# Moving work between engines at the head of an attention and gated feed-forward kernel: normalisation shared with ScalarE, second products placed behind their own unit, the weights' check moved to the end

## The chip, the cores and the metric

One core of one Trainium2 chip runs the whole program. The metric is the device time of one execution in microseconds (us). The engines are TensorE (PE, whose weight loads are listed as PEld), VectorE (DVE), ScalarE (ACT), GpSimd (POOL) and SyncE (SP), which issues nearly all DMAs. Every engine works through its own queue of instructions in order; semaphores hold an instruction until what it reads is ready.

## What is computed

```
scores = q k^T / 8 + bias(head, distance), kept for the last 96 keys and 8 global ones
a      = exp(scores - max) ;  a = a / (sum(a) + 1e-9) ;  x = a v      (4 x 8 heads x 768 x 64)
h      = relu(x @ w_in)                                               (4 x 768 x 1024)
gate   = sigmoid(conv over 3 neighbouring rows of h, weights conv_w)
out    = (h * gate) @ w_out                                           (4 x 768 x 512)
```

The weights arrive as 64-bit floats. The kernel decodes them on the chip from their two 32-bit words, and checks that every high word lies in the range that the short decoding covers; a flag at the very end chooses a general path if one does not. The profiled path is the fast one.

## The kernel before

A *unit* is half of one batch's rows: 384 rows, 8 units (n = 0 to 7). Attention runs in 96 *steps*: step s handles 128 query rows of one pair of heads, three steps make one pair (m), and twelve steps make a unit. In step s PE computes the scores of both heads into one PSUM tile (`scores`, tile s, two buffers), DVE adds the bias and takes the minimum of the negated scores (`maxima`, L378), ACT takes the exponential with its sum (`exps`, L390, into one of three buffers pbuf). `normalise` then runs: DVE adds 1e-9 to the two sums (L398) and takes the reciprocals (L399), POOL multiplies head 0 and head 1 (L402, twice). PE transposes the result (t, L410 and L411), ACT evacuates it (pt, L417), and every third step PE multiplies by v (pv, L433), with ACT and DVE splitting the result into a high and a low part (xh L445, xl L446).

A unit's feed-forward work is built by `ffn(n)` as a list of pieces, which `fill` spreads over the following twelve steps. First products: for each of eight feature blocks f, 12 matmuls (h, L464; tile h1_0 is unit 1, block 0), then relu on ACT (hbuf, L474). The convolution `conv` follows some blocks later: one multiply on POOL (L510), two multiply-adds on DVE (L511, L512). `gate` is a tanh on ACT for two blocks at a time (L530) and `saturated` a test of it, also on ACT (L541). `split` multiplies by h on DVE (L563, tile c), rounds to a high part on ACT (gh, L565) and subtracts on DVE (gl, L566). Second products `mm2`: 24 matmuls for each tile of 128 rows (o, L575; tile o0_2 is batch 0, rows 256 to 383), evacuated by ACT (ob) and stored.

Before the change, `ffn(n)` holds the second products of the tiles that unit n - 1 has completed. Unit 0 has none of its own behind it, so the rest of its convolutions, gates and splits is kept in a list `late` and handed to unit 1's first products, one piece per block. Unit 1's list then contains tiles o0_0 and o0_1, unit 2's list the four tiles o0_2 to o0_5.

Steps 0 to 10 stand in the order in which the code was written (`manual_schedule`); from step 11 on a scheduler of the library orders each engine's queue. Lists of chores ("dve", "pool", "act") are worked off with a budget in every step. They decode the 16 pieces of the weights (w_in first, then w_out: DVE L290, L292, L294, POOL L299, DVE L305), each loaded by SP in 512 KB (tile wr, four buffers). The "act" chores check each piece while it lies there: `piece_check` squares the high words with their sum (L312) and clamps the squares (L315). `check_weights` and `check_gates` turn the results into the flag.

Of the kernel before, what the change touches and what calls it, by code (L numbers as in the profile page):

```python
# [20 lines left out]
P = 128  # L21
# [14 lines left out]
NPB = 3  # L36
HAND = 11
# [25 lines left out]
def fast_path(tc, io):  # L63
# [243 lines left out]
    def piece_check(i, half, n):  # L307
        k = 2 * i + half
        if n == 0:
            squares[k] = p1.tile([P, HW], F32, tag="ob", name=f"square{k}")  # L310
            x = wraw[i, half][:, :, 1].bitcast(F32)
            A.activation(squares[k], x, AF.Square, accum_out=chk[:, NCHK + k : NCHK + k + 1])  # L312
        else:
            y = squares[k]
            A.activation(  # L315
                y, y, AF.Relu, bias=least, scale=-(2.0**30), accum_out=chk[:, k : k + 1]
            )

    squares = {}
# [65 lines left out]
    def exps(s):  # L385
        m, i = steps[s]
        sp, c0, n, mm = st_s[s]
        pb = pbuf[s % NPB]
        for j in range(2):
            last_exp[s] = A.activation(  # L390
                pb[:, j, c0 : c0 + n], sp[j][:, c0 : c0 + n], AF.Exp,
                bias=mm[:, j : j + 1], scale=-1.0, accum_out=mm[:, 2 + j : 3 + j],
            )
        st_s[s] = (pb, c0, n, mm)

    def normalise(s):
        pb, c0, n, mm = st_s[s]
        V.tensor_scalar(mm[:, 4:6], mm[:, 2:4], 1.0e-9, None, ALU.add)  # L398
        V.reciprocal(mm[:, 6:8], mm[:, 4:6])  # L399
        for j in range(2):  # L400
            x = pb[:, j, c0 : c0 + n]
            G.tensor_scalar(x, x, mm[:, 6 + j : 7 + j], 1.0, ALU.mult, ALU.mult)  # L402
# [189 lines left out]
    late = []  # L592

    def ffn(n, defer=True):
        items = []
        add = lambda cost, fn, *a: items.append((cost, fn, a))
        early, lag = late[:], 1 + len(late) // 2
        late.clear()
        for f in range(NF):
            for part in range(3):  # L600
# [17 lines left out]
        old = tiles_of(n - 1) if n else []  # L618
# [43 lines left out]
    chores = {"dve": [], "pool": [], "act": []}  # L662
# [50 lines left out]
    for s in range(len(steps) + LAG_V + 1):  # L713
        cur["s"] = s
        m, i = steps[s] if s < len(steps) else (len(jobs), -1)
        if s < HAND:
# [26 lines left out]
            work("act", 0.8)  # L743
        else:
# [53 lines left out]
    fill(10**9)  # L798

# [14 lines left out]
    def general():  # L814
# [27 lines left out]
        for n in range(NU):  # L842
# [31 lines left out]
            for _, fn, a in ffn(n, defer=False):  # L874
                fn(*a)
# [98 lines left out]
```

## Time and profile before

| what | value |
|---|---|
| median of 3 runs | 479.29 us (476.66, 479.29, 855.67) |
| the profiled execution | 476.23 us, of which the traced span is 474.4 us |
| mean granted TensorE clock in it | 0.959 |
| PE, DVE, ACT, POOL busy, share of the span | 96%, 75%, 62%, 53% |
| HBM read and written | 44.68 MB and 6.29 MB |

The shares are averages over stages with different limits. Matmuls overlap in PE's pipeline, and their ends are modelled, so that a PE which is busy all the time may still wait between matmuls. Tables by stretches of time therefore tell more here than the shares.

### The profile page before, as it was taken

How to read it: one execution, taken by the hardware profiler on the slowest of the kernel's cores; microseconds unless marked ns; L12 is line 12 of the kernel's file. 1: busy time of each engine (PE TensorE's matmuls, PEld its weight loads, DVE VectorE, ACT ScalarE, POOL GpSimd, SP SyncE). 2: the span in 40 equal slices, each digit the busy share in tenths (PEclk: the TensorE clock that was granted, in tenths of full speed). 3: DMA queues.
4: the chain of work that ended last, by engine and by line, in shares of the span. 5: the costliest groups of instructions: out<-in, count | busy, mean ns of one | idle time of the engine just before them, and what ended most of it. 6: DMA issues, size and time to landing. Idle time of an engine off the chain costs nothing.

```text
span 474.4 us, 8982 instructions
## 1 busy us (share of the span) xinstructions
PE 453.7 (96%) x3013; PEld 388.4 (82%) x3013; DVE 355.9 (75%) x936; ACT 293.4 (62%) x806; POOL 250.1 (53%) x351
## 2 busy tenths in 40 slices
PE   7989999969988999999999999999999999999994
PEld 6756688759866899888988998889988998899883
DVE  5889879995998999875798997866798877225600
ACT  2658767875947767754677677654677496335410
POOL 4544364873795597354766766555666754012000
PEclk8877599989998999999999999999999999999999
DMA  7856944223323433243324413433324201100111
GB/s 192 225 158 181 307 121 128 85 86 109 114 100 110 136 123 102 88 123 131 108 80 154 149 55 102 148 125 132 113 75 145 81 1 56 46 24 0 44 46 51
DMA packets 19062, 51.63 MB, mean 109 GB/s; under 512 B 2624, under 2 KB 2880, under 8 KB 19008
## 3 DMA queue, kind: packets, MB, share of 16 engines
q1 hardware_dynamic: 15552, 44.82, 31.0%
q10 hardware_dynamic: 3456, 6.16, 3.4%
q8 instruction: 26, 0.43, 0.4%
q14 instruction: 28, 0.23, 0.2%
HBM read 44.68 MB, written 6.29 MB: 107 GB/s over the span
## 4 chain that ended last, share of the span: by engine, by line
PE 77%; DVE 15%; ACT 2%; issue 2%; POOL 1%; DMA 1%; SPq 0%; POOLq 0%; DVEq 0%; ACTq 0%
PE o L575 26%; PE h L464 25%; PE pv L433 9%; PE s L361 5%; PE s L351 4%; PE t L410 4%; PE t L411 3%; DVE s L378 2%; DVE gl L566 1%; DVE c L511 1%; ACT pbuf L390 1%; DVE c L512 1%; DVE c L563 1%; DMA rq<-in_qk 1%; POOL pbuf L402 1%
## 5 line engine op out<-in xcount | busy, mean ns | idle before, releaser
L402 POOL TENSOR_SCALAR pbuf<-pbuf,mm 128x232 f32<-128x232 f32 (+1 forms) x192 | 137.6, 728 | 88.6 <-DVE mm L399 60.7
L390 ACT ACTIVATE pbuf<-s,mm 128x232 f32<-128x232 f32 (+1 forms) x192 | 83.5, 440 | 62.7 <-DVE mm L378 38.5
L378 DVE CUSTOM_DVE_ANT_0 s<-s,tab 128x232 f32<-128x232 f32 (+1 forms) x192 | 73.6, 385 | 24.6 <-PE s L361 16.9
L575 PE MATMUL o<-woh,gh 128*128 128x512 f32 x192 | 77.4, 403 | 0.0
L575 PE MATMUL o<-wol,gh 128*128 128x512 f32 x192 | 76.4, 398 | 0.0
L575 PE MATMUL o<-woh,gl 128*128 128x512 f32 x192 | 75.7, 395 | 0.0
L510 POOL TENSOR_SCALAR c<-hbuf,cw 128x382 f32<-128x382 f32 (+1 forms) x64 | 47.8, 751 | 51.5 <-ACT hbuf L474 51.5
L433 PE MATMUL pv<-pt,v 104*64 104x128 f32 (+2 forms) x768 | 57.4, 292 | 3.0 <-ACT pt L417 2.7
L464 PE MATMUL h<-xh,wih 128*128 128x384 f32 x252 | 59.8, 350 | 0.0
L464 PE MATMUL h<-xl,wih 128*128 128x384 f32 x252 | 59.2, 343 | 0.0
L464 PE MATMUL h<-xh,wil 128*128 128x384 f32 x252 | 57.9, 343 | 0.0
L433 PEld LDWEIGHTS pv<-pt,v 104*64 104x64 f32 (+2 forms) x768 | 43.2, 142 | 17.4 <-issue 10.0
L511 DVE SCALAR_TENSOR_TENSOR c<-hbuf,cw,c 128x382 f32<-128x382 f32 (+1 forms) x64 | 43.8, 691 | 16.6 <-POOL c L510 16.3
L417 ACT ACTIVATE pt<-t 128x512 f32<-128x512 f32 x80 | 48.0, 603 | 12.1 <-PE t L411 11.9
L410 PE MATMUL t<-ident,pbuf 128*128 128x128 f32 (+1 forms) x192 | 51.3, 286 | 3.9 <-POOL pbuf L402 3.3
L411 PE MATMUL t<-ident,pbuf 128*128 128x128 f32 x192 | 50.4, 281 | 0.0
L474 ACT ACTIVATE hbuf<-h 128x384 f32<-128x384 f32 x64 | 31.8, 498 | 25.8 <-PE h L464 25.7
L512 DVE SCALAR_TENSOR_TENSOR c<-hbuf,cw,c 128x382 f32<-128x382 f32 (+1 forms) x64 | 45.3, 711 | 0.5
L464 PEld LDWEIGHTS h<-xl,wih 128*128 128x128 f32 x252 | 44.2, 188 | 1.8 <-issue 1.8
L464 PEld LDWEIGHTS h<-xh,wih 128*128 128x128 f32 x252 | 44.0, 192 | 1.9 <-issue 1.6
L464 PEld LDWEIGHTS h<-xh,wil 128*128 128x128 f32 x252 | 44.0, 188 | 0.6 <-issue 0.5
L575 PEld LDWEIGHTS o<-woh,gl 128*128 128x128 f32 x192 | 36.3, 189 | 7.5 <-issue 0.2
(107 smaller groups left out, 858.5 us busy)
## 6 DMA issues: line engine op xcount, KB each, us to landing
v<-in_vv SPq DMA_DIRECT2D x32, 384.0 KB, 3.3
rq<-in_qk SPq DMA_DIRECT2D x23, 384.0 KB, 3.2
wr<-in_w SPq DMA_DIRECT2D x16, 512.0 KB, 5.0
rk<-in_qk SPq DMA_DIRECT2D x12, 504.0 KB, 3.5
out<-ob ACTq DMA_DIRECT2D x23, 256.0 KB, 2.0
rk<-in_qk SPq DMA_DIRECT2D x11, 408.0 KB, 3.7
rq<-in_qk SPq DMA_DIRECT2D x9, 192.0 KB, 6.0
rk<-in_qk SPq DMA_DIRECT2D x5, 204.0 KB, 5.9
```

Of the source, the lines that this page charges most:

```text
L378: last_ttr[s] = V.tensor_tensor_reduce(out=sp[j][:, c0 : c0 + n], in0=sp[j][:, c0 : c0 + n], in1=tb, scale=-0.125, scalar=3.0e38, op0=ALU. ...
L390: last_exp[s] = A.activation(pb[:, j, c0 : c0 + n], sp[j][:, c0 : c0 + n], AF.Exp, bias=mm[:, j : j + 1], scale=-1.0, accum_out=mm[:, 2 + ...
L402: G.tensor_scalar(x, x, mm[:, 6 + j : 7 + j], 1.0, ALU.mult, ALU.mult)
L410: T.transpose(pt[:ka, j, 0, :], pb[:, j, c0:P], ident)
L411: T.transpose(pt[:, j, 1, :], pb[:, j, P:256], ident)
L417: last_ev[s] = A.activation(sb, pt, AF.Copy)
L433: T.matmul(pv[m][64 * j : 64 * j + 64, i * P : (i + 1) * P], vt[m][:n, i, c, 64 * j : 64 * j + 64], sb[:n, j, c, :], start=c == 0, stop=c ...
L464: T.matmul(ps[:, :TB], w_[:, k, fs], x_, start=part == 0 and k == 0, stop=part == 2 and k == NK - 1,)
L510: G.tensor_scalar(c, *tap(1), 1.0, ALU.mult, ALU.mult)
L511: V.scalar_tensor_tensor(c, *tap(0), c, ALU.mult, ALU.add)
L512: V.scalar_tensor_tensor(c, *tap(2), c, ALU.mult, ALU.add)
L575: T.matmul(ps, g_[:, f], w_[:, f], start=f == 0 and part == 0, stop=f == NF - 1 and part == 2,)
```

## The change

Five things change, and the amount of arithmetic for the output does not.

1. In steps 0 to 39 (`SHARED = 40`) ACT adds the 1e-9 behind the exponentials, and ACT instead of POOL multiplies head 1. DVE keeps the reciprocal, POOL keeps head 0.
2. In the hand-written steps `normalise(s - 1)` stands behind `maxima(s)` and `exps(s)`.
3. The list `late` is gone. Unit 0's list ends with its own gates and splits and its own tiles o0_0 and o0_1; unit 1's with its own gates, splits and tiles o0_2 and o0_3; unit 2's holds o0_4 and o0_5. From unit 3 on nothing changes.
4. The check leaves the early steps. Behind the last step the high words are loaded again, 16 loads of 512 KB into three freed buffers; for each DVE takes the smallest square (as a maximum of the negated squares), ACT the sum of squares, and one such piece follows every three pieces of PE work.
5. The constant 1.5 becomes the constant 1e-9.

```diff
+SHARED = 40
+CHECK_EVERY = 3
...
-    def piece_check(i, half, n):
-        k = 2 * i + half
-        if n == 0:
-            squares[k] = p1.tile([P, HW], F32, tag="ob", name=f"square{k}")
-            x = wraw[i, half][:, :, 1].bitcast(F32)
-            A.activation(squares[k], x, AF.Square, accum_out=chk[:, NCHK + k : NCHK + k + 1])
-        else:
...
+    def check_load():
+        k = len(words)
+        X, tag = ((p2, "kk"), (p2, "kk"), (p1, "rk"))[k % 3]
+        t = X.tile([P, HW, 2], I32, tag=tag, name=f"check{k}")
+        nc.sync.dma_start(t, weight_words(*divmod(k, 2)))
+        words.append(t[:, :, 1].bitcast(F32))
+
+    def check_piece(k):
+        x = words[k]
+        junk = p2.tile([P, HW], F32, tag="qh", name=f"junk{k}")
+        j2 = p2.tile([P, HW], F32, tag="ql", name=f"junkb{k}")
+        V.tensor_tensor_reduce(
+            out=junk, in0=x, in1=x, scale=-1.0, scalar=-3.0e38,
+            op0=ALU.mult, op1=ALU.max, accum_out=chk[:, k : k + 1],
+        )
+        A.activation(j2, x, AF.Square, accum_out=chk[:, NCHK + k : NCHK + k + 1])
+        if len(words) < NCHK:
+            check_load()
...
+        if s < SHARED:
+            A.activation(mm[:, 4:6], mm[:, 2:4], AF.Identity, bias=eps)
 
     def normalise(s):
         pb, c0, n, mm = st_s[s]
-        V.tensor_scalar(mm[:, 4:6], mm[:, 2:4], 1.0e-9, None, ALU.add)
+        if s >= SHARED:
+            V.tensor_scalar(mm[:, 4:6], mm[:, 2:4], 1.0e-9, None, ALU.add)
         V.reciprocal(mm[:, 6:8], mm[:, 4:6])
         for j in range(2):
-            x = pb[:, j, c0 : c0 + n]
-            G.tensor_scalar(x, x, mm[:, 6 + j : 7 + j], 1.0, ALU.mult, ALU.mult)
+            x, inv = pb[:, j, c0 : c0 + n], mm[:, 6 + j : 7 + j]
+            if j and s < SHARED:
+                A.activation(x, x, AF.Copy, scale=inv)
+            else:
+                G.tensor_scalar(x, x, inv, 1.0, ALU.mult, ALU.mult)
...
-        early, lag = late[:], 1 + len(late) // 2
-        late.clear()
+        lag = 1
...
-        old = tiles_of(n - 1) if n else []
+        old, own = tiles_of(n - 1) if n else [], []
+        if n < 3:
+            old = [[], [], [(0, 4), (0, 5)]][n]
+            own = [[(0, 0), (0, 1)], [(0, 2), (0, 3)], []][n]
...
-        if not mm and defer:
-            late.extend(post[lag:])
-            return items + post[:lag]
         if not mm:
-            return items + post
+            return items + post + [(1, mm2, (b, t, f)) for b, t in own for f in range(NF)]
...
+    def check_some(cost):
+        pace[0] += cost
+        while pace[1] < NCHK and pace[0] >= CHECK_EVERY * (pace[1] + 1):
+            check_piece(pace[1])
+            pace[1] += 1
...
-            if s:
-                normalise(s - 1)
             maxima(s)
             exps(s)
+            if s:
+                normalise(s - 1)
...
+        if s == len(steps):
+            for k in range(3):
+                check_load()
```

How the order of the queues moves is shown at three places. The first is PE where unit 0's first products have ended (h0_7 is the last of them) and the scores of steps 28 and 29 stand (s28, s29); pv7 is the product with v of pair 7. Before:

```order
L464 MATMUL h1_1_1418<-xh6_1240,wih_185 128x384
L433 MATMUL pv7_1308<-pt23_1253,v7_1089 64x128 x4
L433 MATMUL pv7_1308<-pt21_1150,v7_1089 64x128 x4
L433 MATMUL pv7_1308<-pt22_1210,v7_1089 64x128 x4
L361 MATMUL s29_1404<-kk9_1225,qh9_1223 128x232
L361 MATMUL s29_1404<-kk9_1225,ql9_1224 128x232
L361 MATMUL s29_1404<-kk9_1225,qh9_1223 128x232
L361 MATMUL s29_1404<-kk9_1225,ql9_1224 128x232
L464 MATMUL h1_2_1442<-xh4_966,wih_185 128x384
```

After, at the same place:

```order
L448 MATMUL pv7_1343<-pt22_1239,v7_1095 64x128 x4
L370 MATMUL s28_1384<-kk9_1252,qh9_1250 128x232
L370 MATMUL s28_1384<-kk9_1252,ql9_1251 128x232
L370 MATMUL s28_1384<-kk9_1252,qh9_1250 128x232
L370 MATMUL s28_1384<-kk9_1252,ql9_1251 128x232
L590 MATMUL o0_0_1192<-woh_187,gh0_0_1177 128x512
L590 MATMUL o0_0_1192<-wol_188,gh0_0_1177 128x512
L590 MATMUL o0_1_1311<-woh_187,gh0_1_1182 128x512
L590 MATMUL o0_1_1311<-wol_188,gh0_1_1182 128x512
L479 MATMUL h1_0_1418<-xh4_959,wih_185 128x384
```

Unit 0's second products now stand ahead of unit 1's first products, which used to start before step 29; before, o0_0 began behind step 34. Between the scores of steps 29 and 30 the new queue holds 44 matmuls of o0_0 and o0_1, 17 of h1_0 and h1_1, one pv and eight transposes. The next place like it is step 40, behind whose scores o0_2 and o0_3 stand, ahead of unit 2's first products; before, they stood from step 45 on.

The second place is ACT's queue around step 18 (mm17 and mm18 hold the sums and reciprocals of those steps, pbuf0 and pbuf2 their exponentials). Before:

```order
L390 ACTIVATE pbuf0_192,mm18_900<-s18_897,mm18_900 128x232 x2
L474 ACTIVATE hbuf_189<-h0_2_909 128x384
L445 ACTIVATE xh4_966<-pv4_914 128x384
L417 ACTIVATE pt16_935<-t16_930 128x512
L417 ACTIVATE pt17_979<-t17_974 128x512
L530 ACTIVATE c0_882<-c0_882 128x2x382
```

After:

```order
L399 ACTIVATE pbuf0_192,mm18_887<-s18_884,mm18_887 128x232 x2
L460 ACTIVATE xh4_959<-pv4_902 128x384
L405 ACTIVATE mm18_887<-mm18_887,misc_180 128x2
L415 ACTIVATE pbuf2_194<-pbuf2_194,mm17_847 128x232
L432 ACTIVATE pt16_923<-t16_918 128x512
L415 ACTIVATE pbuf0_192<-pbuf0_192,mm18_887 128x232
L489 ACTIVATE hbuf_189<-h0_3_925 128x384
L545 ACTIVATE c0_835<-c0_835 128x2x382
```

ACT has gained the add (L405) and the two multiplications (L415), each of which waits for a reciprocal on DVE, ahead of a relu and a gate.

The third place is DVE behind the last step, where unit 7's convolution (c7) begins; xl31 belongs to the last pair of heads. Before:

```order
L566 TENSOR_TENSOR gl3_2_5069<-c6_4609,gh3_2_5068 128x8x126
L446 TENSOR_TENSOR xl31_5061<-pv31_5032,xh31_5060 128x384
L511 SCALAR_TENSOR_TENSOR c7_5120<-hbuf_189,cw_184,c7_5120 128x386
L512 SCALAR_TENSOR_TENSOR c7_5120<-hbuf_189,cw_184,c7_5120 128x386
L511 SCALAR_TENSOR_TENSOR c7_5120<-hbuf_189,cw_184,c7_5120 128x386
```

After:

```order
L322 ISA junk12_5238,misc_180<-check12_5168 128x512
L322 ISA misc_180 128x1
L526 SCALAR_TENSOR_TENSOR c7_5126<-hbuf_189,cw_184,c7_5126 128x386
L527 SCALAR_TENSOR_TENSOR c7_5126<-hbuf_189,cw_184,c7_5126 128x386
L526 SCALAR_TENSOR_TENSOR c7_5126<-hbuf_189,cw_184,c7_5126 128x386
L322 ISA junk13_5262,misc_180<-check13_5193 128x512
```

Thirteen of the sixteen check pieces stand ahead of the first convolution of unit 7, the last three between its convolutions.

More of the change, by code (lines that the diff above doesn't have):

```diff
@@ L216, in fast_path @@
     odd, red, flag = rest[:, 0:3], rest[:, 3:7], rest[:, 7:8].bitcast(I32)
-    bad, ones, ebias, gbias, least = (rest[:, k : k + 1] for k in range(8, 13))
+    bad, ones, ebias, gbias, eps = (rest[:, k : k + 1] for k in range(8, 13))
     G.memset(gbias, -0.96)
-    G.memset(least, 1.5)
+    G.memset(eps, 1.0e-9)
     def limits():
@@ L305, in weight_low @@
         V.tensor_tensor(l[:, sl], t, h[:, sl].bitcast(F32), ALU.subtract)
-    def piece_check(i, half, n):
-        k = 2 * i + half
-        if n == 0:
-            squares[k] = p1.tile([P, HW], F32, tag="ob", name=f"square{k}")
-            x = wraw[i, half][:, :, 1].bitcast(F32)
-            A.activation(squares[k], x, AF.Square, accum_out=chk[:, NCHK + k : NCHK + k + 1])
-        else:
[L314 to L319, printed above, removed]
+    words = []
+    def check_load():
[15 more added lines that the diff above has]
+            check_load()
     def check_weights():
         small, large = chk[:, :NCHK], chk[:, NCHK:]
-        V.tensor_scalar(small, small, 0.0, None, ALU.is_gt)
+        V.tensor_scalar(small, small, -1.5 * 2.0**-30, None, ALU.is_gt)
         V.tensor_scalar(large, large, 2.0**30, None, ALU.is_le)
@@ L590, in mm2, with ffn @@
             nc.scalar.dma_start(out[b, t * P : (t + 1) * P, :], o)
-    late = []
-    def ffn(n, defer=True):
+    def ffn(n):
         items = []
         add = lambda cost, fn, *a: items.append((cost, fn, a))
-        early, lag = late[:], 1 + len(late) // 2
-        late.clear()
+        lag = 1
         for f in range(NF):
@@ L606, in ffn @@
                 if part == 1:
-                    if early:
-                        items.append(early.pop(0))
                     if f >= lag:
@@ L645, in fast_path @@
     queue, cur = [], {}
+    pace = [0, 0]
+    def check_some(cost):
[3 more added lines that the diff above has]
+            pace[1] += 1
     last_exp, last_mm, last_ev = {}, {}, {}
@@ L660, in fill @@
                 k -= cost
-    chores = {"dve": [], "pool": [], "act": []}
+                if words:
+                    check_some(cost)
+    chores = {"dve": [], "pool": []}
     def work(eng, budget):
@@ L676, in piece_bits @@
         weight_bits(i, half, n)
-        if n == 0:
-            for k in range(2):
-                chores["act"].append((cur["s"], 0.9, piece_check, (i, half, k)))
         if n == 2:
@@ L721, in fast_path @@
                 transposes(s - LAG_T)
+            maxima(s)
+            exps(s)
             if s:
                 normalise(s - 1)
-            maxima(s)
-            exps(s)
             if ends(s - LAG_V - 1):
@@ L742, in fast_path @@
             work("pool", 1.3)
-            work("act", 0.8)
         else:
@@ L779, in fast_path @@
                     work("pool", 1.2)
-                    work("act", 0.8)
+        if s == len(steps):
+            for k in range(3):
+                check_load()
         if s == 0:
@@ L798, in fast_path @@
     fill(10**9)
+    assert pace[1] == NCHK
     def last_tiles():
@@ L873, in general @@
                 xt[m] = (xh, xl)
-            for _, fn, a in ffn(n, defer=False):
+            for _, fn, a in ffn(n):
                 fn(*a)
```

## The prediction

> **What bounds the kernel now.** I read the busy times first, then a table by stretches, because the change touches the first 40 steps and the end.
>
> ```profile
> PE 453.7 (96%) x3013; PEld 388.4 (82%) x3013; DVE 355.9 (75%) x936; ACT 293.4 (62%) x806; POOL 250.1 (53%) x351
> ...
> 8.20:46.40 38.20, 34.82 (x241) 25.31 (x239) 31.84 (x110) 24.90 (x88) 20.42 (x47) 0.77 0.73 204
> 46.40:62.30 15.90, 15.90 (x75) 10.95 (x72) 12.73 (x42) 12.56 (x39) 7.09 (x13) 0.59 0.90 272
> 62.30:91.50 29.20, 29.20 (x198) 24.01 (x200) 27.59 (x78) 20.86 (x61) 17.38 (x26) 1.00 0.29 88
> 91.50:105.60 14.10, 10.18 (x64) 8.09 (x60) 13.50 (x37) 10.93 (x36) 11.41 (x16) 0.94 0.39 124
> 105.60:117.10 11.50, 11.50 (x84) 10.90 (x84) 6.32 (x19) 5.39 (x15) 3.57 (x6) 0.92 0.31 105
> 117.10:138.50 21.40, 20.81 (x156) 18.19 (x155) 20.91 (x54) 17.09 (x51) 18.01 (x19) 1.00 0.38 124
> 138.50:163.80 25.30, 22.00 (x148) 18.03 (x147) 22.64 (x53) 19.16 (x48) 15.92 (x19) 0.93 0.33 103
> 163.80:198.10 34.30, 33.88 (x246) 30.54 (x245) 31.49 (x77) 23.85 (x65) 23.73 (x29) 1.00 0.30 95
> 397.00:435.20 38.20, 38.20 (x231) 34.33 (x230) 16.10 (x24) 16.26 (x29) 7.97 (x10) 1.00 0.08 29
> ```
>
> The columns behind the time are busy us (and instructions) of PE, PEld, DVE, ACT and POOL, the granted clock, the DMA share and GB/s. From 163.8 us on PE is busy throughout at full clock. Ahead of that another engine sets the pace: DVE is busy 31.84 of 38.20 us in the first stretch, 27.59 of 29.20 and 13.50 of 14.10 later, while PE idles 3.9 us in 91.5 to 105.6 and 3.3 us in 138.5 to 163.8. The exception is 46.4 to 62.3, where PE works without a pause at a clock of 0.59. Which steps lie where is told by the reciprocals, one for each step:
>
> ```profile
> 0.00:62.20 62.20, 2.60 (x16) 0.75 0.76 212
> 62.20:92.60 30.40, 1.24 (x8) 1.00 0.30 89
> 92.60:165.20 72.60, 2.54 (x16) 0.95 0.35 113
> 165.20:388.00 222.80, 8.47 (x53) 1.00 0.34 109
> ```
>
> Steps 0 to 15 end at 62 us, 16 to 23 at 93 us, 24 to 39 at 165 us, 40 to 92 by 388 us. At step 40 both versions have done the same PE work: first products of units 0 and 1 and tiles o0_0 and o0_1. What is left, 22 tiles and six units, is the same too, and PE bounds it. So **the question is when step 40 comes**, and whether PE then runs on at once.
>
> **The change, part by part.** Durations:
>
> ```profile
> L402 POOL TENSOR_SCALAR pbuf<-pbuf,mm 128x232 f32<-128x232 f32 x160 | 119.3, 757 | 73.3 <-DVE mm L399 46.5 <-ACT pt L417 6.6 <-ACT pbuf L390 6.6
> L398 DVE TENSOR_SCALAR mm<-mm 128x2 f32<-128x2 f32 x96 | 24.4, 254 | 22.7 <-ACT pbuf L390 22.4
> L390 ACT ACTIVATE pbuf<-s,mm 128x232 f32<-128x232 f32 x160 | 71.8, 455 | 43.9 <-DVE mm L378 24.0 <-PE t L411 12.2 <-POOL pbuf L402 3.4
> L390 ACT ACTIVATION_READ_ACCUMULATOR pbuf<-s,mm 128x1 f32 x192 | 39.1, 204 | 0.0
> L417 ACT ACTIVATE pt<-t 128x512 f32<-128x512 f32 x80 | 48.0, 603 | 12.1 <-PE t L411 11.9
> L530 ACT ACTIVATE c<-c 128x764 f32<-128x764 f32 x16 | 13.8, 864 | 6.6 <-DVE c L512 6.4
> L541 ACT ACTIVATE sat<-c,misc 128x764 bf16<-128x764 f32 x16 | 15.4, 962 | 0.0
> L563 DVE SCALAR_TENSOR_TENSOR c<-c,hbuf 128x1024 f32<-128x1024 f32 x17 | 21.8, 1319 | 2.1 <-ACT sat L541 2.1
> L566 DVE TENSOR_TENSOR gl<-c,gh 128x1024 fp32r<-128x1024 f32 x17 | 21.0, 1241 | 4.7 <-ACT gh L565 4.5
> L565 ACT ACTIVATE gh<-c 128x1024 fp32r<-128x1024 f32 x17 | 18.1, 1072 | 3.8 <-PE o L575 3.4 <-DVE c L563 0.2
> L565 ACT ACTIVATE gh<-c 128x16 fp32r<-128x16 f32 x3 | 0.7, 245 | 0.0
> L312 ACT ACTIVATE square<-wr 128x512 f32<-128x512 f32 x16 | 10.8, 676 | 0.1
> L315 ACT ACTIVATE square<-square,misc 128x512 f32<-128x512 f32 x16 | 11.5, 720 | 0.2
> L378 DVE CUSTOM_DVE_ANT_0 s<-s,tab 128x232 f32<-128x232 f32 x160 | 63.9, 401 | 20.6 <-PE s L361 14.3 <-PE s L351 3.7 <-POOL pbuf L402 1.2
> L378 DVE CUSTOM_DVE_ANT_0 s<-s,tab 128x136 f32<-128x136 f32 x32 | 9.7, 302 | 4.0 <-PE s L361 2.6 <-PE s L351 0.6
> ```
>
> *Sums and head 1.* DVE loses 40 adds of 254 ns, 10.2 us in all. POOL loses 40 of its multiplications, 40 x 757 ns = 30.3 us. ACT gains 40 multiplications of a 128x232 tile; the exponential of that shape, also with an operand from memory, takes 455 ns, and I take that. The add on 128x2 is not in the trace: the read of an accumulator (204 ns) and a copy of 128x16 (245 ns) bound it, I take 230. That is 40 x 0.685 = 27.4 us. In the same steps ACT loses 16 pieces of check at 676 + 720 + two reads of about 200 = 1.8 us, 28.7 us. ACT's load stays as it was.
>
> *Steps 0 to 15.* DVE saves 0.254 us in each. In steps 0 to 11 it sets the pace, 12 x 0.254 = 3.0 us; in 12 to 15 PE at 0.59 does, and a saving on DVE is worth nothing there. Head 1 becomes ready later, because the reciprocal now stands behind the next step's maxima, but the transposes trail by two steps. I take **-2.5 us** (0 to -4).
>
> *Steps 16 to 39.* DVE is busy 27.59 + 13.50 + 6.32 + 20.91 + 22.64 = 91.0 of the 101.5 us from 62.3 to 163.8, and idle 10.5. The adds take 24 x 0.254 = 6.1 us off. What it does otherwise is the same, moved: all of unit 0's convolutions and splits stand ahead of step 29 now. POOL's lighter load also speeds DVE up, as these rows show:
>
> ```profile
> 81.99 0.89 POOL L402 TENSOR_SCALAR pbuf<-pbuf,mm 128x232 f32<-128x232 f32 x2 [1.32 <-DVE mm L398]
> 83.56 1.83 POOL L402 TENSOR_SCALAR pbuf<-pbuf,mm 128x232 f32<-128x232 f32 x2 [0.67 <-DVE mm L399]
> ...
> 99.72 0.96 DVE L511 SCALAR_TENSOR_TENSOR c<-hbuf,cw,c 128x382 f32<-128x382 f32 x1
> 101.76 0.60 DVE L511 SCALAR_TENSOR_TENSOR c<-hbuf,cw,c 128x382 f32<-128x382 f32 x1
> ```
>
> The same pair of multiplications on POOL took 0.89 us and 1.83 us, the same multiply-add on DVE 0.96 us and 0.60 us: each engine is slowed at times, and I read that as the two slowing each other. POOL loses 24 x 757 ns = 18.2 us in this stretch; if half of it lay beside slowed work, DVE gains at most 9.1 x 0.36/0.96 = 3.4 us. I take 1.5 (0 to 3.4). The busy time becomes 91.0 - 6.1 - 1.5 = 83.4 us.
>
> DVE's waits move to other places. (a) Around step 27 the last gate of unit 0 now stands in front of everything: 0.86 for the gate, 0.60 for an evacuation ahead of the exponential, 0.46 + 0.20 for that, then the scores, and 0.96 + 0.20 for the test ahead of the splits; 3.3 us with little other DVE work queued in between: 3 us idle. (b) Between the scores of steps 29 and 30 PE has 44 second and 17 first products. These two rows of the chain price them, 32.70/144 = 0.227 us and 16.66/96 = 0.174 us:
>
> ```profile
> 418.58 16.66 PE h L464 x96
> 435.25 32.70 PE o L575 x144
> ```
>
> 44 x 0.227 + 17 x 0.174 = 12.9 us, while DVE has queued only the last piece of w_out (whose low part o0_0's last block waits for), two subtractions for a new pair and one convolution, which I estimate at 8 us: 5 us idle. (c) Steps 30 to 35 bring 5.5 blocks of first products, 66 x 0.174 = 11.5 us beside scores and transposes: 1.5 us idle. (d) Ahead of unit 1's splits DVE waits 1 us for the last test. Together 10.5 us, as before: two long waits of before (PE's row of first products at 105.6 to 117.1, and the end of unit 1) have given way to two others. 83.4 + 10.5 = 94 against 101.5: **-7.5 us** (-13 with a third of the waits gone and the full 3.4; +3 with twice the waits).
>
> *Behind step 39.* Before, PE lacked 3.3 us of work in 138.5 to 163.8. Now 48 second products (10.9 us) stand ready behind step 40's scores: -2. Against it, three transposes and steps 36 to 39, where PE has only scores, transposes and pv, may cost a stretch of halved clock. The clocks of 0.94 over 14.1 us and 0.92 over 11.5 us amount to (0.06 x 14.1 + 0.08 x 11.5)/0.5 = 3.5 us at half speed after such a pause, worth 1.7 us. Sum **+1** (-2 to +3).
>
> *The check at the end.* 16 squares on ACT cost 16 x 0.88 = 14 us. DVE's reduction over 512 elements is not in the trace; the two shapes of L378 give (401 - 302)/96 = 1.03 ns an element, so 401 + 280 x 1.03 = 690 ns, and with a read as on ACT 0.89 us, 14.3 us for 16 (an estimate; 401 ns alone would make 6.4, twice the slope 19). From 397 to 435 us DVE is busy 16.1 of 38.2 and ACT 16.3: both fit, under PE's work. What can matter is when the loads land, and how much delay unit 7 bears:
>
> ```profile
> wr<-in_w SPq DMA_DIRECT2D x16, 512.0 KB, 5.0
> 442.45 2.44 DVE L566 TENSOR_TENSOR gl<-hbuf,gh 128x16 fp32r<-128x16 f32 x3
> ```
>
> Three buffers and 5.0 us to land, plus the piece itself, give 16/3 x 5.9 = 31 us, from about 386 (step 92's scores, whose reciprocal is taken by 388, free the first buffer) to 417, just ahead of unit 7's first product at 418.58. The last pieces stand between its convolutions. On SP the last pair's v now stands behind the first of these loads; its product is due some 20 us later. Unit 7's splits end at 444.9, and PE asks for the second of these tiles at 435.25 + 72 x 0.227 = 451.6, for the first at 446.2. So 1 to 4 us of delay are covered. I take **+0.5** (0 to +4, where the loads need 7 us).
>
> Sum: 476.23 (the profiled execution, span 474.4) - 2.5 - 7.5 + 1 + 0.5 = 467.7, **468 us**. The median of the three runs is 479.29, the lowest 476.66; 2% of these, 9.5 us, is about what a measurement of this kernel can tell from no change.
>
> **Rivals.** *The new waits eat the gain.* If the chain at the end of units 0 and 1 lies open, each unit pays gate 0.86, test 1.16, split 1.32, gh 1.07, gl 1.24 = 5.7 us without cover; the idle time rises from 10.5 to about 18 us and the time is **476 us**. For it: the orders show PE with nothing but scores, transposes and pv in steps 24 to 27 and 36 to 39. Against it: in both places DVE has a long row of unrelated subtractions and maxima to do. On the clock, the profile shows 0.89 to 0.94 in the stretches with pauses. The Trainium skill, "TensorE: Matmul & The Clock Gate", section "What's actually happening", says that an idle window of about 3.4 us halves TensorE's clock until a window is busy again; the 3.5 us found above agree, and by that rule two open pauses here would cost 1.7 to 3.4 us each, which speaks against gathering PE's waits in one place.
>
> *DVE gains more.* Where a third of the waits goes and the multiply-adds and their like speed up in full, and PE's clock in 46 to 62 us stays up (15.9 us at 0.59), the terms are -4, -13 and +1: **460 us**. The Trainium skill, "GPSIMD Engine Reference", section "1. Specifications", says that POOL shares its SBUF interfaces with VectorE, with contention when DVE reads two SBUF operands or runs in its two-port modes. The 0.96 against 0.60 us agree as far as they go, and by it every multiplication taken off POOL is worth something on DVE.
>
> *ACT becomes the bound: slower.* ACT now holds head 1's multiplication in its queue, and behind it stand relus, gates and exponentials.
>
> ```profile
> POOL pbuf L402 <- DVE mm L399: 27.1, 21, 2.8
> ```
>
> In 8 to 163.8 us POOL waited 27.1 us for these reciprocals, some 16 of them in the last 24 steps. ACT was busy 20.86 + 10.93 + 5.39 + 17.09 + 19.16 = 73.4 us there; less six checks (10.8) and with 24 x 0.685 = 16.4 it comes to 79. Of 94 us that leaves 15, so that inherited waits of 16 us are the point where ACT begins to decide. If they double, 79 + 32 = 111, 17 us over: **485 us**, and more with each wait behind a wait. Against it: ACT may be asked later than POOL was, since its queue is longer.
>
> *It doesn't do what it says*: the orders show every part in place, so I give this nothing.
>
> **Chances.** 468 (463 to 473): 0.45. New waits, 476 (473 to 481): 0.25. More gain, 460 (455 to 463): 0.18. ACT, 485 and above: 0.12. Faster by over 2% (under about 468): 0.18 and half of the first, 0.41. Slower by over 2%: most of the last, 0.10. Within: 0.49. The range leaves out the far parts of the last two: 456 to 482.
>
> **What would show it.** The 40th reciprocal comes near 155 us instead of 165; DVE's busy time from step 16 to 39 falls to about 83 us; L402's successor has 152 instructions; PE pauses around steps 26 and 38; DVE's junk pieces end by 428 and the last second products run without a gap. The forecast is wrong if ACT shows long waits for reciprocals, if the clock falls to half behind both pauses for several windows, or if a check's load holds unit 7's convolutions.

## Result: 1.2% slower where 468 us had been forecast

Over all runs the changed kernel's median is 485.05 us, that of before in the same rounds 478.17 us. The ratio is **1.012 (95% interval 1.0088 to 1.0152)**. By the bound of 2% that is no change, but it lies outside the forecast range of 456 to 482 and on the other side of 1. Several of these kernels have a second group of times some 10 us longer, at a lower granted clock; ratios here come from the faster group of each. The profiled execution took 484.54 us with a span of 482.6, against 476.23 and 474.4.

The page's busy times, and the table by the stretches that the prediction used (columns as there: PE, PEld, DVE, ACT, POOL, granted clock, DMA share, GB/s):

```profile
PE 455.5 (94%) x3013; PEld 390.4 (81%) x3013; DVE 358.0 (74%) x928; ACT 307.2 (64%) x854; POOL 233.1 (48%) x311
```

```profile
8.20:46.40 38.20, 33.95 (x231) 25.38 (x230) 27.52 (x99) 23.67 (x86) 17.49 (x35) 0.79 0.84 228
46.40:62.30 15.90, 15.21 (x111) 11.53 (x111) 15.01 (x44) 12.63 (x41) 7.84 (x11) 1.00 0.82 243
62.30:91.50 29.20, 28.73 (x203) 23.74 (x201) 27.91 (x74) 24.16 (x69) 18.25 (x21) 1.00 0.30 94
91.50:105.60 14.10, 9.83 (x53) 7.90 (x54) 11.47 (x25) 10.35 (x28) 3.48 (x5) 0.64 0.43 140
105.60:117.10 11.50, 11.02 (x57) 9.01 (x56) 10.92 (x23) 6.43 (x23) 7.81 (x8) 1.00 0.30 88
117.10:138.50 21.40, 21.40 (x158) 19.18 (x157) 10.35 (x29) 13.55 (x41) 7.53 (x11) 1.00 0.28 92
138.50:163.80 25.30, 20.46 (x130) 16.63 (x129) 23.20 (x54) 22.24 (x62) 14.62 (x13) 0.74 0.39 122
163.80:198.10 34.30, 34.30 (x228) 31.28 (x228) 20.66 (x60) 17.92 (x49) 16.42 (x22) 1.00 0.26 82
397.00:435.20 38.20, 38.20 (x237) 32.97 (x232) 23.76 (x57) 25.75 (x63) 6.06 (x11) 1.00 0.68 231
```

Three things have changed places. In 46 to 62 us the clock is at 1.00 where it was at 0.59, and DVE works through. In 91.5 to 105.6 and in 138.5 to 163.8 it is the other way round: 0.64 and 0.74 where it was 0.94 and 0.93, and PE idles 4.3 and 4.8 us. In 117 to 138 us DVE is busy 10.35 us of 21.4, where it was busy 20.91.

Aligned by steps instead (first maxima of step 16 to those of step 40, split at steps 24, 28, 30 and 35), before and after:

```profile
62.30:163.80 101.50, 93.69 (x642) 79.22 (x643) 90.95 (x237) 73.44 (x207) 66.29 (x83) 0.97 0.33 106
```

```profile
58.70:89.60 30.90, 30.90 (x215) 25.95 (x215) 28.80 (x77) 25.85 (x75) 17.86 (x23) 1.00 0.33 108
89.60:107.00 17.40, 12.51 (x72) 9.71 (x67) 14.68 (x34) 12.80 (x37) 6.58 (x7) 0.71 0.38 119
107.00:125.20 18.20, 17.86 (x108) 14.71 (x109) 11.35 (x25) 7.96 (x24) 7.88 (x9) 1.00 0.33 107
125.20:143.20 18.00, 18.00 (x131) 17.21 (x130) 13.18 (x36) 13.07 (x40) 9.42 (x14) 1.00 0.29 89
143.20:164.90 21.70, 16.86 (x103) 12.85 (x102) 19.63 (x45) 19.89 (x57) 11.25 (x9) 0.69 0.38 121
58.70:164.90 106.20, 96.13 (x619) 80.44 (x618) 87.65 (x211) 79.56 (x230) 53.00 (x59) 0.89 0.34 109
```

Steps 0 to 15 gained 3.6 us (step 16 at 58.7 instead of 62.3), and the steps behind them gave it back: 106.2 us instead of 101.5. DVE is busy 3.3 us less and idle 8 us more. Its long waits stand in the rows of the timeline (the bracket is the idle time ahead, and what ended it):

```profile
100.89 0.31 DVE L387 CUSTOM_DVE_ANT_0 s<-s,tab 128x136 f32<-128x136 f32 x1 [1.87 <-PE s L370]
120.94 0.56 DVE L461 TENSOR_TENSOR xl<-pv,xh 128x384 fp32r<-128x384 f32 x1 [2.61 <-ACT xh L460]
125.15 0.31 DVE L387 CUSTOM_DVE_ANT_0 s<-s,tab 128x136 f32<-128x136 f32 x1 [3.66 <-PE s L370]
```

The last two lie in the row of second products between the scores of steps 29 and 30: PE reaches one pv and then the scores only behind it. The last rows of the chain:

```profile
425.31 16.64 PE h L479 x96
441.95 33.76 PE o L590 x144
```

Unit 7's first products begin 6.7 us later than before (418.58), the end comes 8.2 us later. So the loss is made of -3.6 to step 16, +4.7 to step 40, +5.6 to unit 7 and +1.5 at the end.

### The profile page after: what moved, and what is told of

It is laid out like the page before. It is cut to its first block, busy times and chain, and to the rows that moved or that the text cites. A ratio compares the mean times of both kernels' runs of the same rounds, so it can differ in the third digit from the quotient of the medians.

```text
span 482.6 us, 8979 instructions
## 1 busy us (share of the span) xinstructions
PE 455.5 (94%) x3013; PEld 390.4 (81%) x3013; DVE 358.0 (74%) x928; ACT 307.2 (64%) x854; POOL 233.1 (48%) x311
## 5 line engine op out<-in xcount | busy, mean ns | idle before, releaser
L417 POOL TENSOR_SCALAR pbuf<-pbuf,mm 128x232 f32<-128x232 f32 (+1 forms) x152 | 114.5, 762 | 82.9 <-DVE mm L411 55.6
L399 ACT ACTIVATE pbuf<-s,mm 128x232 f32<-128x232 f32 (+1 forms) x192 | 83.4, 440 | 54.6 <-DVE mm L387 27.1
L525 POOL TENSOR_SCALAR c<-hbuf,cw 128x382 f32<-128x382 f32 (+1 forms) x64 | 50.4, 789 | 73.8 <-ACT hbuf L489 73.7
L425 PE MATMUL t<-ident,pbuf 128*128 128x128 f32 (+1 forms) x192 | 52.5, 292 | 10.1 <-POOL pbuf L417 5.2
L432 ACT ACTIVATE pt<-t 128x512 f32<-128x512 f32 x80 | 47.9, 601 | 18.1 <-PE t L426 17.1
L590 PEld LDWEIGHTS o<-woh,gh 128*128 128x128 f32 x192 | 36.7, 191 | 8.2 <-ACT gh L580 1.0
```

What stands on the lines that cost most here:

```text
L399: last_exp[s] = A.activation(pb[:, j, c0 : c0 + n], sp[j][:, c0 : c0 + n], AF.Exp, bias=mm[:, j : j + 1], scale=-1.0, accum_out=mm[:, 2 + ...
L417: G.tensor_scalar(x, x, inv, 1.0, ALU.mult, ALU.mult)
L425: T.transpose(pt[:ka, j, 0, :], pb[:, j, c0:P], ident)
L432: last_ev[s] = A.activation(sb, pt, AF.Copy)
L525: G.tensor_scalar(c, *tap(1), 1.0, ALU.mult, ALU.mult)
L590: T.matmul(ps, g_[:, f], w_[:, f], start=f == 0 and part == 0, stop=f == NF - 1 and part == 2,)
```

## Experiments

Part 3 alone was not put on the kernel before: the early check's squares share the buffer "ob" with the evacuations that part 3 brings forward, and as the code reads, the two would wait for each other in that order. So the parts were taken away from the changed kernel.

**Which part loses.** Run e1 restores the list `late` and the old places of the tiles; e2 sets `SHARED = 0` and puts `normalise` back; e3 does both, which leaves part 4; e4 has parts 1 and 2 on the kernel before.

```diff
 # e1, against the changed kernel (e3: this and e2's edit)
-        lag = 1
+        early, lag = late[:], 1 + len(late) // 2
+        late.clear()
...
-        if n < 3:
-            old = [[], [], [(0, 4), (0, 5)]][n]
-            own = [[(0, 0), (0, 1)], [(0, 2), (0, 3)], []][n]
...
+        if not mm and defer:
+            late.extend(post[lag:])
+            return items + post[:lag]
 # e2, against the changed kernel
-SHARED = 40
+SHARED = 0
...
 # e4, against the kernel before
+        if s < SHARED:
+            A.activation(mm[:, 4:6], mm[:, 2:4], AF.Identity, bias=eps)
...
```

> The changed kernel with part 3 undone: unit 0's last convolutions, gates and splits go back to the list late, o0_0 and o0_1 back to unit 1's list, o0_2 to o0_5 to unit 2's. Sharing with ScalarE (parts 1 and 2) and the check at the end stay. Theory A (part 3 loses: it gathers PE's waits at steps 24 to 27 and 36 to 39, halves the clock there and then leaves VectorE idle behind long rows of second products): the gain of the hand-written steps, 3.6 us at step 16, stays, and the time is 0.985 to 0.997 of before; less than 10 us at half clock after 90 us. Theory B (sharing loses, because ScalarE waits in order for reciprocals): still 1.008 to 1.015 of before. Theory C (the check at the end loses): 1.008 to 1.015, with the loss behind step 92. Theory D (any new order of the queues moves the time by about 1%, without adding up): 0.99 to 1.015, with the loss at places that no part touches.

> The changed kernel with parts 1 and 2 undone: no step is shared with ScalarE, and normalise stands ahead of maxima in the hand-written steps. Own tiles (part 3) and the check at the end (part 4) stay. Theory A: slower than the changed kernel, since the loss stays and the gain is gone: 1.012 to 1.025 of before, with over 15 us at half clock after 90 us. Theory B: 0.99 to 1.003. Theory C: 1.008 to 1.015 with the loss behind step 92. Theory D: anything from 0.995 to 1.02.

> The kernel before with part 4 alone: the early check is gone, the check stands behind the last step. Theories A and B: ScalarE has 28.7 us less to do in the first 40 steps, and the tail costs nothing: 0.993 to 1.002 of before, relu of unit 7's block 0 to the end 53 to 55 us as before (53.7). Theory C: 1.008 to 1.015, and that stretch is 58 us or longer.

> The kernel before with parts 1 and 2 alone: 40 steps shared with ScalarE, normalise behind maxima and exps in the hand-written steps; the check stays in the early steps, beside the shared work. Theory A: 0.985 to 0.998 of before (VectorE's 10 us less to do partly turned into time). Theory B: 1.005 to 1.02, with ScalarE waiting over 20 us for reciprocals. Where ScalarE's load as such matters (sharing pays only where the check has left), this is slower than the run without own tiles by 3 us or more.

| run | times, us | ratio to before (95%) |
|---|---|---|
| e1, without own tiles | 468.4, 468.9, 469.3 and 478.8, 480.2, 480.7 | 0.981 (0.974 to 0.989) |
| e2, without sharing | 479.3 to 497.9, median 489.1 | none |
| e3, check at the end alone | 478.3, 485.3 to 486.8, 497.5 | none |
| e4, sharing alone | 479.6 to 495.8, median 482.3 | 1.010 (1.006 to 1.013) |

Theory A holds for e1 in its direction: without part 3 the change is faster than before, by a little more than the 0.985 to 0.997 that was expected, and no stretch behind 90 us is at half clock. e2 and e3 settle nothing by their times, which reach over more than 18 us each. Table by steps 16 to 39, and by steps 12 to 15, of e1:

```profile
59.70:152.80 93.10, 87.00 (x623) 74.32 (x622) 84.62 (x209) 75.84 (x228) 49.33 (x59) 1.00 0.38 117
46.80:59.70 12.90, 12.22 (x95) 8.81 (x95) 12.84 (x39) 10.53 (x35) 6.52 (x9) 1.00 0.93 278
```

DVE is busy 84.62 and idle 8.5 in 93.1 us. The prediction had 83.4, 10.5 and 94: **its sum was that of the change without part 3**, to the end (468.4 profiled, 468 forecast). That is in part luck, for the waits in that sum were reasoned out for the changed order, which e1 doesn't have. For e4 theory A is wrong: sharing alone is slower than before. The same two tables of e4, and steps 12 to 15 of e3:

```profile
46.60:65.20 18.60, 18.32 (x88) 12.65 (x87) 12.16 (x36) 13.28 (x45) 5.23 (x9) 0.56 0.60 149
65.20:164.00 98.80, 91.81 (x621) 76.89 (x622) 85.39 (x214) 84.86 (x256) 50.17 (x58) 0.97 0.39 123
```

```profile
47.00:65.60 18.60, 16.62 (x75) 11.19 (x76) 12.32 (x40) 4.79 (x16) 7.12 (x12) 0.50 0.63 188
```

In steps 16 to 39 sharing saves DVE 5.6 us of work (6.3 in e1), though ACT, which keeps the check, is busy 84.9 of 98.8 us (75.8 of 93.1 in e1). But steps 12 to 15 took 18.6 us in both, 12.9 in e1, 15.9 before, at a clock of 0.56 (e4), 0.50 (e3), 1.00 and 0.59. ACT's load is not what these steps have in common: it is busy 13.28 us of them in e4 and 4.79 in e3. Theory B has the number of e4 (1.005 to 1.02) but not the mechanism: ACT waited 3.5 us for reciprocals ahead of its multiplications, not over 20. In the profiled run of e4 step 40 comes at 164.0 us, as before (163.8); its 4.6 us of loss lie behind that, and their cause stays open. Theory D, with the clock as its means, became a theory of its own.

**Is it the clock of the early steps?** Theory E was tested by one table, on four of the kernels:

```diff
-WARM = (43, 0, 16, 16, 16, 12, 8, 4, 4, 4, 4, 4)
+WARM = (43, 0, 16, 16, 16, 16, 16, 16, 16, 16, 16, 16)
```

> The kernel before with one table changed: the idle matmuls (warm) that stand on TensorE in steps 5 to 11 are raised from 12, 8, 4, 4, 4, 4, 4 to 16 each, 72 more of 128 columns. Theory E (what moves these kernels most is TensorE's clock in steps 4 to 24: windows of 3.4 us with few columns streamed are followed by windows at half clock, and the next edit shifts them): the halved stretches of 28.9 to 39.1 us and 45.9 to 59.6 us go or shrink to one, step 16 comes by 60 us instead of 62.3, and the time is 0.980 to 0.993 of before with a mean clock of 0.975 or more. If the clock only follows waits that are there anyway: the 72 matmuls cost 72 x 0.056 to 0.112 = 4 to 8 us of TensorE in steps that VectorE paces, and the time is 0.998 to 1.012.

> The changed kernel with the same table of idle matmuls. Theory E with theory A (part 3 loses by its own waits, the clock in the early steps adds to it): early halved stretches go, those at 92 to 103 us and 150 to 164 us stay: 0.995 to 1.008 of before, 3 to 6 us slower than the kernel before with the same table. If the early clock were all: the same as the kernel before with this table, within 2 us.

> The run without own tiles (sharing and the check at the end stay) with the same table. Theory E: no halved stretch between 24 and 150 us in any run, so that its two groups of times (468 to 469 and 479 to 481) become one: 0.970 to 0.984 of before, 3 us or more under the kernel before with this table. Without theory E: 0.982 to 0.995, still in two groups.

> The check at the end alone with the same table. Theory E: its loss (485 us in the profiled run, with 23.9 us at half clock from 46 to 70 us) was the clock's and not the check's, so it becomes the same as the kernel before with this table, within 2 us. If the check at the end costs by itself: still 6 to 10 us over that.

| run | times, us | clock | ratio to before (95%) |
|---|---|---|---|
| e5, before | 480.4 to 485.4 | 0.953 to 0.970 | 1.012 (1.007 to 1.017) |
| e6, changed | 483.5 to 487.0 | 0.959 to 0.973 | 1.016 (1.011 to 1.021) |
| e7, without own tiles | 468.4 to 470.3 | 0.982 to 0.990 | 0.982 (0.978 to 0.987) |
| e8, check at the end | 470.6 to 484.3 | 0.951 to 0.987 | 0.992 (0.987 to 0.996) |

For e7 theory E holds: one group of times, no longer two, with 0.982 inside its range, though one halved stretch of 3.4 us was left at 134 us where none was expected. e6 missed its 0.995 to 1.008; it lies 1.4 us over e5, since e5 got slower too. e8 falls from 486.7 to 475.9 in the median, and its 13 times follow their clock: 470.6 at 0.987, 473.6 to 475.9 at 0.972 to 0.982, 480.5 to 484.3 at 0.951 to 0.962. It was expected within 2 us of e5 or 6 to 10 over it, and lies 8 us under it. So the check at the end is no loss of several microseconds, and theory C falls. For e5 I was wrong: the kernel before got slower with the table, at the upper end of the other branch (0.998 to 1.012), in which the idle matmuls only cost time; its windows from 53 to 67 us stayed at half clock. The idle matmuls are no cure by themselves. In the profiled runs of e6 and e7, which share with ScalarE, no stretch from 16 to 90 us is at half clock; in e5, which doesn't share, 13.7 us are, and e8's clock still differs from run to run. Why was not tested.

With the clock of the early steps steady, part 3 can be priced: 485.07 (e6) against 469.27 (e7), **15.8 us**. Steps 16 to 39 of the two:

```profile
56.20:166.20 110.00, 97.63 (x632) 81.76 (x631) 87.99 (x211) 79.43 (x230) 50.14 (x59) 0.91 0.35 108
```

```profile
56.20:151.40 95.20, 88.98 (x624) 75.85 (x622) 84.37 (x209) 76.06 (x228) 49.16 (x59) 0.98 0.38 116
```

DVE idles 22.0 us in the first and 10.8 in the second. The clock is not the same in them either: behind 90 us e6 has 23.9 us at half clock, e7 3.4. How much of the 15.8 us is DVE's waits and how much the clock, these two runs don't tell.

**Which piece of part 3.** All four with the larger table of idle matmuls:

```diff
 # e9, against the changed kernel
-            old = [[], [], [(0, 4), (0, 5)]][n]
-            own = [[(0, 0), (0, 1)], [(0, 2), (0, 3)], []][n]
+            old = [[], [(0, 0), (0, 1)], [(0, t) for t in (2, 3, 4, 5)]][n]
 # e10
+            old = [[], [], [(0, t) for t in (2, 3, 4, 5)]][n]
+            own = [[(0, 0), (0, 1)], [], []][n]
 # e11 (own tiles also behind a list that has old ones)
+            old = [[], [(0, 0), (0, 1)], [(0, 4), (0, 5)]][n]
+            own = [[], [(0, 2), (0, 3)], []][n]
 # e12, against the changed kernel
+FILL = (24, 25, 26, 27, 36, 37, 38, 39)
...
+                if s in FILL:
+                    wf = ps_m.tile([P, 512], F32, tag="m", name=f"fill{s}")
+                    with tc.issue_after(last_mm[s].ins):
+                        for _ in range(16):
+                            filled[s] = T.matmul(wf[:, :P], wk, wk, start=True, stop=True)
```

> The changed kernel with the larger table of idle matmuls and only the first half of part 3: unit 0's and unit 1's gates and splits stand behind their own first products (no list late), but o0_0 and o0_1 stay in unit 1's list and o0_2 to o0_5 in unit 2's. TensorE's order from step 24 to 42 is then nearly that of the run without own tiles: two blocks of h0 still stand between the scores of steps 24 to 28. Theory A1 (the loss is in the tiles: 48 more pieces in a unit's list pull its first products together, leave TensorE without work ahead of the splits, and put 40 products in one row where VectorE has nothing to do): 466 to 471 us, as without own tiles (469.3 with this table). Theory A2 (the loss is in the early gates and splits): 477 us or more.

> The same with o0_0 and o0_1 at the end of unit 0's list, but o0_2 to o0_5 in unit 2's: the row of 38 second products between the scores of steps 29 and 30 is there, the pause in steps 36 to 39 is not. Theory A1: step 30 comes 10 to 15 us later than without own tiles (105.3), as in the changed kernel with this table (120.5), and some comes back in steps 36 to 40: 475 to 481 us, with a halved clock near 90 to 103 us. If only unit 1's half loses: 468 to 472.

> The same with o0_0 and o0_1 in unit 1's list and o0_2 and o0_3 at its end. Steps 24 to 30 are as without own tiles; the second products stand in rows of 15 to 24 in steps 33 to 40. Theory A1: about half of the loss, 472 to 478 us, and the time of step 30 within 2 us of 105.3. If only unit 0's half loses: 468 to 471.

> The changed kernel with the larger table and 16 idle matmuls of 128 columns behind the scores of each of the steps 24 to 27 and 36 to 39, where it pauses and its clock halves. The scheduler then also puts o0_0 and o0_2 between these scores instead of behind them. Theory F (half of the loss of part 3 is the halved clock behind the pauses): halved stretches of 90 to 110 and 150 to 160 us go, mean clock 0.98 or more, 475 to 480 us instead of 485. If the waits of VectorE are all of it: 484 to 488.

| run | median, us (range) | ratio to before (95%) |
|---|---|---|
| e9, own gates and splits only | 470.2 (468.3 to 472.5) | 0.986 (0.983 to 0.990) |
| e10, and unit 0's tiles | 480.4 (479.4 to 481.5) | 1.007 (1.004 to 1.010) |
| e11, and unit 1's tiles | **466.6** (465.0 to 467.4) | **0.978 (0.975 to 0.980)** |
| e12, changed, with fillers | 489.3 (487.1 to 490.4) | 1.025 (1.022 to 1.028) |

Early gates and splits cost nothing clear of noise (469.3 without them). Unit 0's own tiles cost 10.2 us. Unit 1's own tiles alone, which I had expected to lose 3 to 9 us, gain 3.6. DVE's long waits in e10, and steps 16 to 39 of e11:

```profile
99.19 0.31 DVE L387 CUSTOM_DVE_ANT_0 s<-s,tab 128x136 f32<-128x136 f32 x1 [2.38 <-PE s L370]
119.66 0.31 DVE L387 CUSTOM_DVE_ANT_0 s<-s,tab 128x136 f32<-128x136 f32 x1 [4.76 <-PE s L370]
```

```profile
59.10:156.30 97.20, 93.70 (x651) 79.97 (x650) 86.16 (x212) 78.71 (x233) 47.95 (x60) 1.00 0.37 116
```

In e11 PE has o0_0 and o0_1 in store for the steps in which unit 1's gates and splits are made, and no stretch there has a lower clock. In the changed kernel these two tiles are already gone, and the pause of steps 36 to 39 opens. I read that as the reason why the two pieces don't add (10.2 - 3.6 would leave 476.8, and the changed kernel with this table takes 485.1); no run tests it by itself.

e12 missed as a test of theory F: the scheduler spread o0_0 and o0_1 among the scores of steps 24 to 28, each of which then waited for them. Step 24 alone, and steps 25 to 29:

```profile
90.00:107.70 17.70, 12.52 (x83) 8.74 (x79) 14.23 (x24) 9.62 (x21) 3.45 (x5) 0.81 0.30 92
107.70:128.80 21.10, 21.10 (x163) 17.67 (x164) 9.08 (x30) 11.95 (x39) 8.07 (x11) 1.00 0.26 83
```

The halved stretches of 90 to 110 and 150 to 160 us, which were to go, are still there, 17.1 us instead of 23.9. Its mean clock rose from 0.966 to 0.976 in the profiled runs, and it is 4 us slower all the same, DVE being busy 9.08 us of 21.1 in the second stretch: the order of the products matters beside the clock, and the clock's own share of the loss stays open.

**Why unit 0's tiles lose.** They do two things: 48 more pieces in its list pull its first products together (they end at step 23 instead of 27), and a row of second products stands ahead of unit 1's first products. e13 has the row without the packing, e14 the packing without the row (empty pieces in the list); e15 is e11 with the old table of idle matmuls.

```diff
 # e13, against e11
+        if n == 1:
+            items += [(1, mm2, (0, t, f)) for t in (0, 1) for f in range(NF)]
...
-            old = [[], [(0, 0), (0, 1)], [(0, 4), (0, 5)]][n]
+            old = [[], [], [(0, 4), (0, 5)]][n]
 # e14, against e11
+        if n == 0:
+            post += [(1, lambda: None, ())] * (2 * NF)
```

> Run e11 (unit 1's own tiles) with o0_0 and o0_1 at the front of unit 1's list, ahead of its first products. Unit 0's list keeps its 96 pieces, so that its first products are spread as without own tiles, up to step 27; the 48 second products stand in one row with 64 first products between the scores of steps 34 and 35. Theory R (the row ahead of the first products is what loses): VectorE idles most of that row, 48 x 0.227 + 64 x 0.174 = 22 us less about 8 us of its own work, and 475 to 486 us. Theory P (packing loses: 48 more pieces in unit 0's list end its first products early and leave TensorE a pause in steps 24 to 28): 465 to 470 us.

> Run e11 with 48 empty pieces at the end of unit 0's list, which do nothing: unit 0's first products are packed as in the changed kernel and end at step 23, but o0_0 and o0_1 stay in unit 1's list. Theory P: the pause of steps 24 to 27 and its halved clock come back without the tiles, 474 to 481 us. Theory R: 465 to 470 us, and step 30 no later than 107 us.

> Run e11 with the old table of idle matmuls (12, 8, 4, 4, 4, 4, 4 in steps 5 to 11). Theory E (the larger table only keeps the clock up in steps 8 to 20): the best times are those of e11 (465 to 467) or 1 us better, others 6 to 12 us longer with a lower mean clock, as the run without own tiles had them with this table (468.4 to 469.3 and 478.8 to 480.7).

| run | median, us (range) | ratio to before (95%) |
|---|---|---|
| e13, row without packing | 485.3 (479.7 to 487.0) | 1.014 (1.008 to 1.020) |
| e14, packing without row | 472.0 (470.6 to 474.2) | 0.989 (0.986 to 0.993) |
| e15, e11 with the old table | 469.1 to 470.3, and 478.9, 480.7 | 0.985 (0.981 to 0.989) |

Neither theory holds alone. The row costs 18.7 us over e11, as theory R expected; the packing costs 5.4, and e14 lies between the two forecasts (474 to 481 and 465 to 470). e13's row is longer than the changed kernel's (112 products against 61, because the scheduler gathered more behind it), and 18.7 us is more than the 10.2 of unit 0's tiles in e10. So both effects are shown, but not what each is worth in the changed kernel. That row, with steps 33 and 34 around it, in the table, and DVE's wait in it:

```profile
115.20:142.20 27.00, 27.00 (x137) 24.14 (x134) 13.20 (x28) 12.81 (x34) 9.55 (x11) 0.92 0.21 69
```

```profile
135.03 0.17 DVE L411 RECIPROCAL mm<-mm 128x2 f32<-128x2 f32 x1 [10.66 <-ACT mm L405]
```

PE is busy for 27 us while DVE is busy 13.2; the 48 second products done there are not missed later, since DVE is what bounds the steps that follow. And the pause of the packing in e14, steps 24 to 27:

```profile
90.10:108.00 17.90, 13.18 (x72) 10.75 (x69) 14.65 (x34) 12.70 (x36) 6.08 (x7) 0.62 0.37 111
```

17.9 us at a clock of 0.62, where e11 takes 13.4 us for the same steps. e15 shows what the table of idle matmuls is for: without it two groups of times again, the better one 3 us above e11, where it had been expected level with e11 or 1 us better. **e11 is the version that beats both kernels**: the one before by 2.2% (so near the bound of 2% that the interval covers it), the changed one with the same table of idle matmuls by 3.8% (466.62/485.07 = 0.962, from two sets of rounds).

## Why the prediction was wrong, by its own steps

*Sums and head 1.* The prices were right or small in their misses. Groups of the changed kernel:

```profile
L415 ACT ACTIVATE pbuf<-pbuf,mm 128x232 f32<-128x232 f32 (+1 forms) x40 | 18.5, 467 | 6.7 <-DVE mm L411 6.7
L405 ACT ACTIVATE mm<-mm,misc 128x2 f32<-128x2 f32 x40 | 11.8, 295 | 0.8 <-POOL misc L221 0.3
L322 DVE CUSTOM_DVE_ANT_0 junk<-check 128x512 f32<-128x512 f32 x16 | 11.1, 698 | 11.5 <-DMA check<-in_w 11.5
L326 ACT ACTIVATE junkb<-check 128x512 f32<-128x512 f32 x16 | 10.8, 672 | 7.4 <-DMA check<-in_w 7.3
```

ACT's multiplication took 467 ns (455 taken), its add 295 (230), together 30.3 us instead of 27.4; DVE's check 698 ns (690). In steps 16 to 39 ACT waited 4.3 us for reciprocals ahead of its multiplications and 4.1 ahead of exponentials, about half of the 16 us from which the rival "ACT becomes the bound" decides.

*Steps 0 to 15* gave -3.6 where -2.5 was taken. The reason given, that PE at 0.59 makes DVE's saving worthless in steps 12 to 15, did not last: the clock was at 1.00 from 46 to 62 us in this run.

*Steps 16 to 39* is the step that failed: -7.5 forecast, +4.7 measured, and its term of DVE's waits above all. Its busy time, 83.4 forecast, was 87.65 in the changed kernel and 84.62 in e1, which leaves two of unit 1's long subtractions (1.25 us each) for later. The 1.5 us that POOL's lighter load was to bring did not show: the 32 multiply-adds of these steps took 24.0 us before, 23.3 in the changed kernel, 24.3 in e1 and 24.1 in e4. The idle time was put at 10.5 us; it was 18.5: 2.7 us in steps 24 to 27 for item (a), which had 3; 6.85 in 28 and 29 for (b), which had 5; 4.8 in 30 to 34 for (c), which had 1.5; 2.1 behind that for (d), which had 1; and 2.1 in steps 16 to 23, where none was counted. The reasoning that "two long waits of before have given way to two others" took it that the new waits would be no longer than the old ones; they came to 18.5 us where the old ones had 10.5. It also took the second products of unit 0 for work that PE would be glad to have done. e10 and e13 show that it is not: PE does them while DVE idles, and in the steps that should gain from it DVE is the bound.

*Behind step 39*, +1 forecast, +5.6 measured to unit 7's first product. The largest piece of it falls where unit 3's splits stand: by the reciprocals the changed kernel is 2.7 us behind at step 60 and 6.9 at step 72 (rows of POOL and of PE):

```profile
263.18 5.79 POOL L417 TENSOR_SCALAR pbuf<-pbuf,mm 128x232 f32<-128x232 f32 x4 [3.96 <-DVE mm L411]
```

```profile
268.59 0.33 PE L425 MATMUL t<-ident,pbuf 128*128 128x128 f32 x1 [1.76 <-POOL pbuf L417]
```

Four multiplications took 5.79 us beside DVE's splits, PE waited for the last, and the window behind it ran at half clock. Nothing in the change touches unit 3 but the time at which the scheduler meets it, and I had not looked there; what sets the rest was not followed up. The halved clock ahead of step 40 was foreseen in kind ("a stretch of halved clock", 3.5 us); after 90 us it is 27 us here, 6.8 before.

*The check at the end* had +0.5 (0 to +4) and took +1.5; the junk pieces ended at 437 us, not by 428, and DVE's 11.5 us of waits for their loads were covered. 1.1 us of it is the last row, 144 second products in 33.76 us instead of 32.70; all runs with the check at the end show that spacing, those with the early check the old one, and why stays open.

*The rivals.* "The new waits eat the gain" named the place and the clock, and its idle time, about 18 us, is what came. Its 476 us was 8 short, because DVE's busy time and the part behind step 39 came out 4 us over the forecast each. The Trainium skill's rule, "TensorE: Matmul & The Clock Gate", section "What's actually happening", that an idle window of 3.4 us halves the clock, was cited for two pauses that cost 1.7 to 3.4 us each. The lengths agree with windows of that size (halved stretches of 3.4, 6.8, 10.2 and 13.7 us), but the two stretches in question lasted 10.2 and 13.7 us, where "Behind step 39" had one of 3.5. "DVE gains more" had its clock in 46 to 62 us, but no run shows the faster multiply-adds that it needed.

*What would have shown it*: the 40th reciprocal came at 165.7 us, not near 155 (156.5 in e1):

```profile
0.00:165.85 165.85, 6.17 (x40) 0.88 0.51 148
```

## What to carry to other kernels

Work moved ahead is worth something only where the engine that does it sets the pace afterwards too; ask for the stretch that should become shorter which engine bounds it. Matmuls that are ready and not urgent are stock: keep them for the steps in which the chain of gates and splits leaves TensorE without work, and don't spend them ahead of products that other engines wait for. A list that is spread evenly over steps changes the pace of all that stands ahead in it when something is added at its end.

## What the runs showed of the hardware

The same four steps (12 to 15) took 12.9, 15.9 and 18.6 us at granted clocks of 1.00, 0.59 and 0.50, though the scheduler doesn't put quite the same matmuls into them. PE busy throughout did not always bring the clock back here, and PE need not be idle to lose it. The first two rows are of the kernel before: the 3.41 us ahead of its longest halved stretch and the 10.24 us at its beginning. The other two are the 3.41 us ahead of the two long halved stretches of the changed kernel.

```profile
42.52:45.93 3.41, 2.38 (x15) 1.48 (x15) 2.82 (x9) 3.41 (x14) 1.44 (x2) 1.00 0.77 262
45.93:56.17 10.24, 10.24 (x38) 6.93 (x37) 7.99 (x26) 8.54 (x27) 3.59 (x7) 0.50 0.90 281
```

```profile
89.02:92.43 3.41, 2.06 (x25) 1.51 (x21) 3.29 (x12) 2.43 (x11) 2.73 (x4) 1.00 0.35 97
147.05:150.46 3.41, 2.30 (x23) 1.57 (x20) 3.29 (x12) 3.41 (x14) 1.58 (x2) 1.00 0.65 178
```

In these three windows, after which the clock halved, PE was busy 2.06 to 2.38 of 3.41 us. The Trainium skill's table, "TensorE: Matmul & The Clock Gate", section "What's actually happening", has the half clock after an idle window and the full clock back after one busy window. Here three busy windows in a row did not bring it back. They held scores on 64 rows, products with v on 64 columns, transposes and five first products. What a window has to hold was not measured by itself. The Trainium skill says in the same section that the windows run freely; no run here shows whether that makes the two groups of times of e1 and e15.
